# First feed-forward product of two batches as seven block products for eight, its weight blocks streamed from DRAM, with all engines in written order

## The chip, the core and the metric

The kernel runs on one core of a Trainium2 chip. A core has TensorE (PE in the profile; its weight loads are the row PEld), VectorE (DVE), ScalarE (ACT), GpSimd (POOL) and SyncE (SP), whose queue issues the transfers here. The metric is the device time of one execution in microseconds. "Granted clock" is the share of TensorE's full clock that the chip allowed in a stretch; the two levels are 1.2 and 2.4 GHz.

## The reference

Attention with normalized queries and keys, then a feed-forward layer with a squared ReLU, in fp32. The two weight matrices come as 64-bit floats (a numpy product with a 64-bit scalar made them so), so the kernel also rounds them to 32 bits.

```
# q, k, v: (8, 12, 448, 64); w_in: (768, 2048); w_out: (2048, 768)
q_n, k_n = rmsnorm(q, g_q), rmsnorm(k, g_k)       # over the last axis
scores = (1 / sqrt(64)) * q_n @ k_n^T
attn = exp(scores - max(scores)); attn /= sum(attn) + 1e-9
x = (attn @ v), laid out as (8 * 448, 12 * 64)
g = max(x @ w_in, 0) ** 2
out = g @ w_out                                   # (3584, 768)
```

## The kernel before

The work goes by batch (8) and, in a batch, by pair of heads (6). A pair's q and k come with 112 partitions; `norm` squares them and scales them by the reciprocal root of their mean (POOL, with one sum on DVE), `transposes` brings them into `qkT` with PE and DVE, `scores` makes four tiles of 112 x 2 x 448 scores with one exponential each on ACT (`pr`), `values` multiplies them with v, and POOL adds the four tiles up (`acc`), so that `finish` can get the totals with two matmuls (`tot`), take the reciprocal and write the normalized, transposed output `xT` of the batch.

`feed_forward` of a batch is a generator: 16 pieces of the first product (`ph`, six matmuls of 128x128 weights on 448 columns, then ReLU on ACT and a square in place on POOL into `gT`), then the second product (`po`, 16 matmuls of 384 columns a piece) with its rows copied out by DVE and ACT and stored. Its pieces are dealt out between the half pairs of the next batch's attention; the last batch's feed-forward runs alone. Both weights lie in SBUF as `w1` and `w2`. They are loaded as 64-bit words in 32 pieces, three at a time, and rounded in `round_weights` during the first batch's attention: exponent and fraction are put together on DVE and ACT, and multiplied on POOL.

PE runs in the written order; on the other engines and the queue a scheduler chooses the order. One row of an order listing with `MATMUL` is a matmul of the program; the trace shows two instructions for each fp32 matmul, and one for each transpose.

Of the kernel before, what the change touches and what calls it, by code (L numbers as in the profile page):

```python
# [9 lines left out]
F32 = mybir.dt.float32  # L10
# [294 lines left out]
def attention_then_ffn_bounded(  # L305
# [24 lines left out]

    nc = tc.nc
# [4 lines left out]
    P = 128  # L336
# [5 lines left out]
    REST = S % P  # L342
    FULL = S - REST
    assert 2 * D == P and S % NJ == 0 and SP <= P and B % 2 == 0
    assert DM == H * D and NT == B * S and 2 * REST == P and DFF % 512 == 0
# [3 lines left out]
    work = ctx.enter_context(tc.tile_pool(name="work", bufs=2))  # L349
    small = ctx.enter_context(tc.tile_pool(name="small", bufs=4))  # L350
    ps_s = ctx.enter_context(tc.tile_pool(name="ps_s", bufs=2, space=bass.MemoryType.PSUM))
# [10 lines left out]
    rebias = consts.tile([P, 1], F32, name="rebias")  # L362
# [6 lines left out]
    NW = 768  # L369
    NSET = 3  # L370
    spare = gT.rearrange("p f n -> p (f n)")
    assert NSET * 3 * NW <= NFC * (S + REST)
# [3 lines left out]
    CW = NPAIR // 2  # L376
    FW = NW // CW
    pieces_w = [(w1[:, c:c + CW, f:f + FW], w1r[:, c:c + CW, words_in * f:words_in * (f + FW)])
                for f in range(0, DFF, FW) for c in (0, CW)]
    pieces_w += [(w2[:, c:c + 1, :], w2r[:, c:c + 1, :]) for c in range(NFC)]  # L380

    def raw(n):
        _, a, m = pieces_w[n][0].shape
        at = n % NSET * 3 * NW
        words = spare[:, at:at + 2 * NW].bitcast(U32)
        return words.rearrange("p (a m) -> p a m", a=a), words.rearrange("p (a m two) -> p a m two", a=a, two=2)

    def load_weights(n):
        if n < len(pieces_w):
            nc.sync.dma_start(raw(n)[0] if doubles else pieces_w[n][0], pieces_w[n][1])  # L390

    def round_weights(n):
        if not doubles:
            return
        w = pieces_w[n][0]
        wu = w.bitcast(U32)
        words = raw(n)[1]
        low, high = words[:, :, :, 0], words[:, :, :, 1]
        at = n % NSET * 3 * NW + 2 * NW
        f = spare[:, at:at + NW].rearrange("p (a m) -> p a m", a=w.shape[1])  # L400
        fu = f.bitcast(U32)
        nc.vector.tensor_scalar(wu, high, 20, 0x7FF, ALU.logical_shift_right, ALU.bitwise_and)
        nc.scalar.activation(wu, wu, AF.Relu, bias=rebias)
        nc.vector.tensor_scalar(fu, high, 0xFFFFF, None, ALU.bitwise_and)
        nc.vector.scalar_tensor_tensor(f, low, 2.0 ** -32, fu, ALU.mult, ALU.add)
        nc.scalar.activation(f, f, AF.Copy, bias=1.0, scale=2.0 ** -20)
        nc.vector.tensor_scalar(wu, wu, 255.0, 2.0 ** 23, ALU.min, ALU.mult)  # L407
        nc.vector.scalar_tensor_tensor(wu, high, 0x80000000, wu, ALU.bitwise_and, ALU.bitwise_or)  # L408
        nc.gpsimd.tensor_tensor(w, f, w, ALU.mult)


    qks, vs, qkTs, probs, pavs, accs, xTs = {}, {}, {}, {}, {}, {}, {}
# [14 lines left out]
    normed = {}  # L427

    def norm(i):
        qk = qks.pop(i)  # L430
        qkn = work.tile([SP, 2, NJ, 2, D], F32, tag="qkn", name="qkn", bufs=1)
# [16 lines left out]
    def transposes(i):  # L448
        qkn = normed.pop(i)
        qkT = work.tile([P, 2, S], F32, tag="qkT", name="qkT")  # L450
# [8 lines left out]
    def scores(i, c):  # L459
# [10 lines left out]
        if c == 1:  # L470
            accs[i] = work.tile([SP, 2, S], F32, tag="acc", name="acc")
            nc.gpsimd.tensor_tensor(accs[i], probs[i, 0], pr, ALU.add)  # L472
        elif c > 1:
            nc.gpsimd.tensor_tensor(accs[i], accs[i], pr, ALU.add)  # L474
# [3 lines left out]
    def values(i, cs):  # L478
# [8 lines left out]
    def finish(i):  # L487
        b, hp = divmod(i, NPAIR)
        acc = accs.pop(i)
        tot = ps_o.tile([P, S], F32, tag="t", name="tot")  # L490
        for h in range(2):
            nc.tensor.matmul(tot[h * D:(h + 1) * D, :], ones, acc[:, h, :], start=True, stop=True)  # L492
        rec = work.tile([P, S], F32, tag="rec", name="rec", bufs=1)
        nc.vector.reciprocal(rec, tot)  # L494
        if hp == 0:
            xTs[b] = work.tile([P, NPAIR, S], F32, tag="xT", name="xT")
        nc.vector.tensor_tensor(xTs[b][:, hp, :].rearrange("d (p j) -> d j p", j=NJ),  # L497
                                pavs.pop(i).rearrange("d (j p) -> d j p", j=NJ),
                                rec.rearrange("d (j p) -> d j p", j=NJ), ALU.mult)
        del vs[i]  # L500

    def feed_forward(b):
        xT = xTs.pop(b)
        odd = b % 2
        c0 = 0 if odd else REST
        for f in range(NFC):  # L510
            ph = ps_m.tile([P, S], F32, tag="m", name="ph")
            for c in range(NPAIR):
                nc.tensor.matmul(ph, w1[:, c, f * P:(f + 1) * P], xT[:, c, :],  # L513
                                 start=(c == 0), stop=(c == NPAIR - 1))
            g = gT[:, f, c0:c0 + S]
            nc.scalar.activation(g, ph, AF.Relu)  # L516
            nc.gpsimd.tensor_tensor(g, g, g, ALU.mult)  # L517
            yield
        for t in range(0, FULL + P * odd, P):
            osb = work.tile([P, DM], F32, tag="osb", name="osb")  # L520
            for half in range(2):
                cols = slice(half * HALF, (half + 1) * HALF)
                po = ps_m.tile([P, HALF], F32, tag="m", name="po")
                for f in range(NFC):
                    nc.tensor.matmul(po, gT[:, f, c0 + t:c0 + t + P], w2[:, f, cols],  # L525
                                     start=(f == 0), stop=(f == NFC - 1))
                if half == 0:
                    nc.vector.tensor_copy(osb[:, cols], po)  # L528
                else:
                    nc.scalar.copy(osb[:, cols], po)  # L530
                if half == 1:
                    if t < FULL:
                        nc.sync.dma_start(out[b * S + t:b * S + t + P, :], osb)
                    else:
                        nc.sync.dma_start(out[b * S + FULL:(b + 1) * S, :], osb[0:REST])
                        nc.sync.dma_start(out[(b - 1) * S + FULL:b * S, :], osb[REST:P])
                yield

    def pieces(b):
        return NFC + 2 * (FULL // P + b % 2)  # L540
# [8 lines left out]
    for n in range(NSET):  # L549
        load_weights(n)  # L550
    make_identity(nc, ident)
    nc.gpsimd.memset(mhalf, -0.5)
    nc.gpsimd.memset(rebias, -896.0)
# [5 lines left out]
    NP = B * NPAIR  # L559
    for b in range(B):  # L560
        fill = feed_forward(b - 1) if b else iter(())
        n = pieces(b - 1) if b else 0
        done = 0
        blocks = 2 * NPAIR
        for u in range(blocks):
            i, second = b * NPAIR + u // 2, u % 2
            if not second:
                if i + 2 < NP:
                    load(i + 2)
                scores(i, 0)  # L570
                scores(i, 1)
                if i + 1 < NP:
                    norm(i + 1)
                if u:
                    values(i - 1, (2, 3))
                    finish(i - 1)
            else:
                if i + 1 < NP:
                    load_v(i + 1)
                    transposes(i + 1)  # L580
                scores(i, 2)
                scores(i, 3)
                values(i, (0, 1))
            if b == 0:
                m = len(pieces_w)
                for n_w in range(m * u // blocks, m * (u + 1) // blocks):
                    round_weights(n_w)
                    load_weights(n_w + NSET)
            if u == blocks - 1:
                values(i, (2, 3))  # L590
                finish(i)
            while done < n * (u + 1) // blocks:
                next(fill)
                done += 1
        for _ in fill:
            pass
    for _ in feed_forward(B - 1):
        pass
# [3 lines left out]
def kernel(  # L602
# [31 lines left out]
    with tc.If(bits <= limit) as small_scores:  # L634
        with tc.manual_schedule(engines={mybir.EngineType.PE}):
# [33 lines left out]
```

## Time and profile before

| | us |
|---|---|
| median of 3 runs (lowest to highest) | 1854.67 (1854.55 to 1856.01) |
| the profiled execution | 1852.34 |
| its span from first to last instruction | 1850.5 |
| PE busy in the span | 1624.2 (88%) |
| POOL busy | 833.4 (45%) |
| DVE busy | 496.7 (27%) |
| ACT busy | 304.4 (16%) |
| mean granted TensorE clock | 0.944 |

Busy time is a mean over stages. Which engine sets the end of a stage is read from the stretches, the chain that ended last (followed back from the last instruction to what released each step), and the idle time in front of an instruction, with the engine that ended it. Ends of matmuls are modelled, so the distance from start to start is the safer measure on PE.

### The profile page before, as it was taken

The page shows a single profiled execution, that of the slowest core. Times are in us where ns is not written, and L with a number is a line of the kernel's source. Part 1 is how long each engine was busy: PE and PEld are TensorE (multiplying, and loading weights), DVE is VectorE, ACT ScalarE, POOL GpSimd, SP SyncE. Part 2 cuts the span into 40 slices and gives each one's busy share as a digit, 9 for nine tenths or more (in the row PEclk, how much of TensorE's full clock was granted, in tenths as well). Part 3 has the DMA queues.
Part 4 walks back from the last instruction along what each step waited for, and adds up shares of the span by engine and source line. Part 5 has one row for each costly group of instructions (what it writes and reads, how often), then busy time and mean ns, then how long its engine had stood idle before and what let it go on. Part 6 is the DMA issues. An engine that isn't in the chain of part 4 may idle for free.

```text
span 1850.5 us, 13250 instructions
## 1 busy us (share of the span) xinstructions
PE 1624.2 (88%) x5440; PEld 804.5 (43%) x5440; DVE 496.7 (27%) x432; ACT 304.4 (16%) x413; POOL 833.4 (45%) x553
## 2 busy tenths in 40 slices
PE   3242479998999899998999899998999899999998
PEld 1111134454445444454445454454445454455555
DVE  6898941211211211211211212211211212210000
ACT  2333322101120011201120011201120011200100
POOL 6777676622662236622662236622663235601200
PEclk9657679998999999999999999999999999999999
DMA  5433400000100100000100100000100100000000
GB/s 157 135 119 116 148 25 25 20 33 24 30 25 24 37 24 21 25 33 24 30 26 24 37 24 17 29 32 24 30 25 24 37 24 15 10 18 9 0 10 27
DMA packets 47754, 70.16 MB, mean 38 GB/s; under 512 B 3652, under 2 KB 35908, under 8 KB 47684
## 3 DMA queue, kind: packets, MB, share of 16 engines
q1 hardware_dynamic: 47684, 69.22, 12.0%
q8 instruction: 44, 0.72, 0.2%
q14 instruction: 26, 0.21, 0.0%
HBM read 58.20 MB, written 11.01 MB: 37 GB/s over the span
## 4 chain that ended last, share of the span: by engine, by line
PE 81%; POOL 4%; DVE 2%; ACT 1%; issue 0%; POOLq 0%; ACTq 0%
PE po L525 32%; PE ph L513 32%; PE sc L465 7%; PE pav L484 6%; PE tot L492 2%; POOL acc L474 2%; PE pt L454 1%; POOL rstd L439 1%; ACT gT L516 1%; POOL qkn L441 1%; POOL qkn L434 1%; DVE rstd L437 0%; DVE w L407 0%; ACT osb L530 0%; DVE w L408 0%
## 5 line engine op out<-in xcount | busy, mean ns | idle before, releaser
L513 PE MATMUL ph<-xT,w 128*128 128x448 f32 x1536 | 595.6, 544 | 7.6 <-DVE xT L497 7.6
L525 PE MATMUL po<-w,gT 128*128 128x384 f32 x1792 | 592.3, 492 | 0.0
L525 PEld LDWEIGHTS po<-w,gT 128*128 128x128 f32 x1792 | 342.5, 192 | 256.0 <-issue 27.5
L513 PEld LDWEIGHTS ph<-xT,w 128*128 128x128 f32 x1536 | 287.5, 190 | 314.1 <-issue 305.6
L494 DVE RECIPROCAL rec<-tot 128x448 f32<-128x448 f32 x48 | 141.9, 2956 | 554.5 <-PE tot L492 554.5
L517 POOL TENSOR_TENSOR gT<-gT 128x448 f32<-128x448 f32 x128 | 118.3, 933 | 293.9 <-ACT gT L516 293.9
L465 PE MATMUL sc<-qkT 64*112 64x448 f32 x768 | 188.5, 614 | 60.1 <-DVE qkT L456 60.1
L472 POOL TENSOR_TENSOR acc<-pr 112x896 f32<-112x896 f32 x48 | 102.8, 2141 | 287.3 <-ACT pr L468 287.1
L474 POOL TENSOR_TENSOR acc<-acc,pr 112x896 f32<-112x896 f32 x96 | 201.1, 2095 | 27.5 <-ACT pr L468 27.1
L468 ACT ACTIVATE pr<-sc 112x896 f32<-112x896 f32 x192 | 166.9, 913 | 157.5 <-PE sc L465 157.5
L434 POOL TENSOR_TENSOR qkn<-qk 112x1024 f32<-112x1024 f32 x48 | 91.5, 1907 | 201.9 <-PE pt L454 191.7
L516 ACT ACTIVATE gT<-ph 128x448 f32<-128x448 f32 x128 | 69.7, 544 | 596.4 <-PE ph L513 596.4
L484 PE MATMUL pav<-pr,vt 112*64 112x448 f32 x768 | 167.4, 561 | 0.0
L456 DVE TENSOR_SCALAR qkT<-pt,gains 128x448 f32<-128x448 f32 x96 | 65.3, 682 | 340.0 <-PE pt L454 338.9
L454 PE MATMUL pt<-ident,qkn 112*128 112x112 f32 x384 | 62.1, 289 | 98.0 <-POOL qkn L441 88.5
L439 POOL TENSOR_TENSOR rstd<-rstd,mhalf 112x16 f32<-112x16 f32 x48 | 139.7, 2911 | 3.8
L465 PEld LDWEIGHTS sc<-qkT 64*112 64x112 f32 x768 | 67.1, 189 | 141.8 <-issue 133.5
L530 ACT COPY osb<-po 128x384 f32<-128x384 f32 x28 | 13.4, 479 | 682.3 <-PE po L525 682.3
L528 DVE COPY osb<-po 128x384 f32<-128x384 f32 x28 | 15.6, 558 | 349.2 <-PE po L525 349.2
L441 POOL TENSOR_TENSOR qkn<-qk,rstd 112x512 f32<-112x512 f32 x96 | 101.7, 1063 | 3.6
L454 PEld LDWEIGHTS pt<-ident,qkn 112*128 112x128 f32 x384 | 45.3, 153 | 132.2 <-POOL qkn L441 83.0
L484 PEld LDWEIGHTS pav<-pr,vt 112*64 112x64 f32 x768 | 48.3, 139 | 115.1 <-issue 90.2
(27 smaller groups left out, 497.4 us busy)
## 6 DMA issues: line engine op xcount, KB each, us to landing
gT<-in_moe_w_in_dram SPq DMA_DIRECT2D x16, 768.0 KB, 4.8
gT<-in_moe_w_out_dram SPq DMA_DIRECT2D x16, 768.0 KB, 4.3
qk<-in_q_dram SPq DMA_DIRECT2D x48, 224.0 KB, 2.9
qk<-in_k_dram SPq DMA_DIRECT2D x48, 224.0 KB, 3.2
vt<-in_v_dram SPq DMA_DIRECT2D x48, 224.0 KB, 2.7
out_dram<-osb SPq DMA_DIRECT2D x24, 384.0 KB, 2.3
out_dram<-osb SPq DMA_DIRECT2D x8, 192.0 KB, 2.7
gains<-in_g_q_dram SPq DMA_DIRECT2D x2, 0.2 KB, 2.9
```

Of the source, the lines that this page charges most:

```text
L434: nc.gpsimd.tensor_tensor(sq, flat, flat, ALU.mult)
L439: nc.gpsimd.tensor_tensor(rflat, rflat, mhalf, ALU.pow)
L441: nc.gpsimd.tensor_tensor(qkn[:, s].rearrange("p j h d -> p h j d"), qk[:, s].rearrange("p h (j d) -> p h j d", d=D), rstd[:, s].rearrange ...
L454: nc.tensor.transpose(pt[:, j * SP:(j + 1) * SP], qkn[:, s, j].rearrange("p h d -> p (h d)"), ident[:SP, :SP])
L465: nc.tensor.matmul(sc[:, h, 0:S], qkT[rows, 1, c * SP:(c + 1) * SP], qkT[rows, 0, :], start=True, stop=True)
L468: nc.scalar.activation(pr, sc[:, :, 0:S], AF.Exp)
L474: nc.gpsimd.tensor_tensor(accs[i], accs[i], pr, ALU.add)
L484: nc.tensor.matmul(pavs[i][h * D:(h + 1) * D, :], vs[i][:, h, c, :], pr[:, h, :], start=(c == 0), stop=(c == NJ - 1))
L494: nc.vector.reciprocal(rec, tot)
L513: nc.tensor.matmul(ph, w1[:, c, f * P:(f + 1) * P], xT[:, c, :], start=(c == 0), stop=(c == NPAIR - 1))
L517: nc.gpsimd.tensor_tensor(g, g, g, ALU.mult)
L525: nc.tensor.matmul(po, gT[:, f, c0 + t:c0 + t + P], w2[:, f, cols], start=(f == 0), stop=(f == NFC - 1))
```

## The change

Two batches make a span. With the weights cut in two halves each way (rows and columns of `w_in`) and the output of attention cut by features and by batch, the first product is a 2 x 2 block product; it is written with 7 block products and 15 additions (Strassen's scheme in Winograd's form). Four differences of the inputs are made on DVE in `finish` (`xC`, and a part of `xT` in place). The seven weight operands of each of 8 block rows (four of them differences, made on POOL) are written once to a DRAM tensor `w1s`, and read back one block (128 x 384) per product through six buffers `sw`. The additions of the results run on DVE, between PSUM and SBUF; three PSUM banks are accumulated into a second time.

A span's attention now runs beside the second product of the span before, cut into single matmuls, 200 of 224 over the 24 half pairs; the first product runs with nothing beside it, except the norm and transposes of one pair and, in the first span, the rounding of `w_out`. At the start, two batches' attention runs beside the rounding of `w_in`; there PE makes the totals from all four probability tiles. The square of `norm` and the copy to `qkT` go to ACT, one of three sums of probabilities to DVE. Every engine and the queue keep the written order.

```diff
-    w1 = consts.tile([P, NPAIR, DFF], F32, name="w1")
...
-    gT = consts.tile([P, NFC, S + REST], F32, name="gT")
+    gT = consts.tile([P, NFC, 2 * S], F32, name="gT")
+    xT = consts.tile([P, 2, NPAIR, S], F32, name="xT")
+    xC = consts.tile([P, 3, HC, S], F32, name="xC")
...
+    def exponents(words, w):
+        wu = w.bitcast(U32)
+        nc.vector.tensor_scalar(wu, pairs_of(words)[1], 20, 0x7FF, ALU.logical_shift_right, ALU.bitwise_and)
+        nc.scalar.activation(w, wu, AF.Relu, bias=clamp1, scale=-1.0)
+        nc.scalar.activation(wu, w, AF.Relu, bias=clamp2, scale=-(2.0 ** 23))
+    def fractions(words, w):
+        low, high = pairs_of(words)
+        wu = w.bitcast(U32)
+        f = low.bitcast(F32)
+        nc.vector.scalar_tensor_tensor(wu, high, 0x80000000, wu, ALU.bitwise_and, ALU.bitwise_or)
+        nc.vector.tensor_scalar(high, high, 0xFFFFF, None, ALU.bitwise_and)
+        nc.vector.scalar_tensor_tensor(f, low, 2.0 ** -32, high, ALU.mult, ALU.add)
+        nc.scalar.activation(f, f, AF.Copy, bias=1.0, scale=2.0 ** -20)
...
+        if step == 2 and n % 2:
+            nc.gpsimd.tensor_tensor(b[S1], b[A21], b[A22], ALU.add)
+            nc.gpsimd.tensor_tensor(b[S2], b[S1], b[A11], ALU.subtract)
+            nc.gpsimd.tensor_tensor(b[S3], b[A11], b[A21], ALU.subtract)
+            nc.gpsimd.tensor_tensor(b[S4], b[A12], b[S2], ALU.subtract)
+        if step == 3 and n % 2:
+            nc.sync.dma_start(w1s[n // 2].rearrange("k p m -> p k m"), w1_blocks(n)[:, 0:7])
...
+    def load_blocks(upto):
+        while len(stream) < min(upto, NSPAN * HF * 7):
+            n = len(stream)
+            sw = loads.tile([P, HC, P], F32, tag="sw", name="sw", bufs=6)
+            nc.sync.dma_start(sw.rearrange("p c m -> p (c m)"), w1s[n // 7 % HF, n % 7])
+            stream.append(sw)
...
-        nc.gpsimd.tensor_tensor(sq, flat, flat, ALU.mult)
+        nc.scalar.activation(sq, flat, AF.Square)
...
-            nc.vector.tensor_scalar(qkT[:, s], pt, gains[:, s:s + 1], None, ALU.mult)
+            nc.scalar.activation(qkT[:, s], pt, AF.Copy, scale=gains[:, s:s + 1])
...
+            nc.gpsimd.tensor_tensor(accs[i], probs[i, 0], pr, ALU.add)
+        else:
+            (nc.vector if c == 2 else nc.gpsimd).tensor_tensor(accs[i], accs[i], pr, ALU.add)
...
+        if t:
+            sub = nc.vector.tensor_tensor
+            if hp < HC:
+                sub(xC[:, 0, hp], xT[:, 1, hp], xT[:, 0, hp], ALU.subtract)
+            else:
+                n = hp - HC
+                sub(xC[:, 1, n], xT[:, 1, hp], xC[:, 0, n], ALU.subtract)
+                sub(xC[:, 2, n], xT[:, 0, hp], xC[:, 1, n], ALU.subtract)
+                sub(xT[:, 1, n], xT[:, 1, hp], xT[:, 1, n], ALU.subtract)
...
+        def product(ps, n, rhs, first):
+            load_blocks(n + 6)
+            for c in range(HC):
+                nc.tensor.matmul(ps, stream[n][:, c], rhs[:, c], start=first and c == 0,
+                                 stop=c == HC - 1, skip_group_check=not first)
...
+            pa = ps_o.tile([P, S], F32, tag="t", name="pa")
+            product(pa, n + A11, B11, True)
+            p1 = work.tile([P, S], F32, tag="p1", name="p1")
+            nc.scalar.copy(p1, pa)
+            yield
+            pb = ps_m.tile([P, S], F32, tag="m", name="pb")
+            product(pb, n + S2, T2, True)
+            z = work.tile([P, S], F32, tag="z", name="z")
+            add(z, p1, pb, ALU.add)
+            yield
...
+            product(pd, n + S3, T3, True)
+            add(g22, y, pd, ALU.add)
+            activate(g22, g22)
+            yield
+            product(pa, n + A12, B21, False)
+            activate(g11, pa)
+            yield
+            product(pd, n + A22, T4, False)
+            add(g21, z, pd, ALU.add)
+            activate(g21, g21)
...
+    for span in range(NSPAN):
...
+            for u, _ in enumerate(first_product(work, span)):
+                if span == 0:
+                    for n in range(4 * u // 7, 4 * (u + 1) // 7):
+                        for step in range(3):
+                            make_w2(n - step, step)
+                if more and u == 7 * (HF - 2):
+                    norm(nxt)
+                if more and u == 7 * (HF - 1):
+                    transposes(nxt)
...
+                each, done = (2 * S // P) * 2 * NFC - 24, 0
+                for u, _ in enumerate(attention(work, span + 1, False)):
+                    while done < each * (u + 1) // NB:
+                        next(rest)
+                        done += 1
...
-        with tc.manual_schedule(engines={mybir.EngineType.PE}):
+        with tc.manual_schedule():
```

In the middle of the kernel before, PE's order for one pair of heads beside the feed-forward of the batch before is this (`pt` transposes, `sc` scores, `pav` values, `tot` totals, `ph` first product):

```order
L454 MATMUL pt<-ident,qkn 128x112 x8
L465 MATMUL sc<-qkT 112x448 x4
L484 MATMUL pav<-pr,vt 64x448 x4
L513 MATMUL ph<-xT,w_100 128x448 x12
L465 MATMUL sc<-qkT 112x448 x4
L484 MATMUL pav<-pr,vt 64x448 x4
L492 MATMUL tot<-acc,ones 64x448 x2
```

After the change, PE's order for one pair of heads in the second span's attention, with the semaphores that an instruction waits for:

```order
L577 MATMUL tot<-acc,ones 64x448 [waits Pool_49]
L577 MATMUL tot<-acc,ones 64x448
L690 MATMUL po<-w_99,gT 128x384 x8
L534 MATMUL pt<-ident,qkn 128x112 [waits DVE_49,Pool_49]
L534 MATMUL pt<-ident,qkn 128x112 x3
L534 MATMUL pt<-ident,qkn 128x112 [waits Activation_49,Pool_49]
L534 MATMUL pt<-ident,qkn 128x112 x3
L545 MATMUL sc<-qkT 112x448 x4
L566 MATMUL pav<-pr,vt 64x448 [waits DMAHW5_49,DVE_49]
L566 MATMUL pav<-pr,vt 64x448 x3
L690 MATMUL po<-w_99,gT 128x384 x6
```

Between the half pairs stand some eight matmuls of the second product where there were two pieces of the feed-forward, and the second four transposes wait for ACT besides POOL.

On ACT, early in the first batch, the order before is this (L403 and L406 the two weight steps of a piece, L468 exponentials):

```order
L403 ACTIVATE w_100<-w_100,rebias 128x3x256
L406 ACTIVATE gT<-gT 128x768
L468 ACTIVATE pr<-sc 112x896 x2
L406 ACTIVATE gT<-gT 128x768
L468 ACTIVATE pr<-sc 112x896
L403 ACTIVATE w_100<-w_100,rebias 128x3x256 x2
```

On ACT, in the first span, the order after the change around one pair (L536 copies to `qkT`, L548 exponentials, L514 the square of `norm`, L391, L392 and L402 the three weight steps of one piece):

```order
L548 ACTIVATE pr<-sc 112x896 x2
L514 ACTIVATE qkn<-qk 112x1024
L391 ACTIVATE gT<-gT,clamp_103 128x768
L392 ACTIVATE gT<-gT,clamp_104 128x768
L402 ACTIVATE gT<-gT 128x768
L536 ACTIVATE qkT<-pt,gains 128x448 x2
L548 ACTIVATE pr<-sc 112x896 x2
L391 ACTIVATE gT<-gT,clamp_103 128x768
L392 ACTIVATE gT<-gT,clamp_104 128x768
L402 ACTIVATE gT<-gT 128x768
```

The copies of a pair now stand behind the weight steps of the half pair before it; before, a scheduler put single weight steps between the exponentials, and ACT had neither the copies nor the squares of the attention.

On SP, around the end of the first span's attention after the change (`w1s` the store of weight blocks, `gT<-in_moe_w_out` a piece of the second weights, `sw` a block):

```order
L506 DMA vt<-in_v_dram 112x2x256
L460 DMA w1s<-gT 128x7x384
L468 DMA gT<-in_moe_w_out_dram 128x1536 x3
L490 DMA sw<-w1s 128x384 x11
L468 DMA gT<-in_moe_w_out_dram 128x1536
L490 DMA sw<-w1s 128x384
L468 DMA gT<-in_moe_w_out_dram 128x1536
```

The first blocks stand behind the last store and three pieces of the second weights; all of these are new at this place.

## Rows read from the trace of the kernel before

**Rows 1.** Busy time by stretch: start to end, engines, then clock, DMA share, GB/s.
```profile
0.00:245.00 245.00, 89.88 (x292) 34.72 (x292) 211.19 (x198) 77.96 (x91) 173.46 (x96) 0.70 0.41 127
245.00:1689.00 1444.00, 1379.12 (x4700) 684.65 (x4700) 283.30 (x231) 215.29 (x301) 645.01 (x442) 0.98 0.08 26
```

**Rows 2.** Chain that ended last: start, length, instructions (us).
```profile
448.16 9.23 PE ph L513 x24
...
865.45 9.23 PE ph L513 x24
...
1689.53 72.16 PE ph L513 x192
1761.69 82.57 PE po L525 x256
```

**Rows 3.** Timeline of PE, 525 to 540 us: start, length, instructions, idle before.
```profile
525.33 1.76 PE L465 MATMUL sc<-qkT 64*112 64x448 f32 x8
527.02 1.72 PE L484 MATMUL pav<-pr,vt 112*64 112x448 f32 x8
528.58 0.92 PE L492 MATMUL tot<-acc,ones 112*64 112x448 f32 x4
529.43 9.29 PE L513 MATMUL ph<-xT,w 128*128 128x448 f32 x24
...
539.35 0.60 PE L454 MATMUL pt<-ident,qkn 112*128 112x112 f32 x4 [0.25 <-ACT gT L516]
```

**Rows 4.** Timeline of PE at the end of a batch's attention.
```profile
840.20 1.76 PE L492 MATMUL tot<-acc,ones 112*64 112x448 f32 x4 [7.95 <-POOL acc L474]
```

**Rows 5.** Groups of attention's instructions by line: busy us, mean ns of one.
```profile
L468 ACT ACTIVATE pr<-sc 112x896 f32<-112x896 f32 x192 | 166.9, 913 | 157.5 <-PE sc L465 157.5
L494 DVE RECIPROCAL rec<-tot 128x448 f32<-128x448 f32 x48 | 141.9, 2956 | 554.5 <-PE tot L492 554.5
L439 POOL TENSOR_TENSOR rstd<-rstd,mhalf 112x16 f32<-112x16 f32 x48 | 139.7, 2911 | 3.8
...
L441 POOL TENSOR_TENSOR qkn<-qk,rstd 112x512 f32<-112x512 f32 x96 | 101.7, 1063 | 3.6
...
L516 ACT ACTIVATE gT<-ph 128x448 f32<-128x448 f32 x128 | 69.7, 544 | 596.4 <-PE ph L513 596.4
...
L456 DVE TENSOR_SCALAR qkT<-pt,gains 128x448 f32<-128x448 f32 x96 | 65.3, 682 | 340.0 <-PE pt L454 338.9
...
L437 DVE TENSOR_REDUCE rstd<-qkn 112x16 f32<-112x1024 f32 x48 | 58.5, 1218 | 60.6 <-POOL qkn L434 60.6
...
L497 DVE TENSOR_TENSOR xT<-pav,rec 128x448 f32<-128x448 f32 x48 | 46.1, 961 | 1.5
...
L438 POOL TENSOR_SCALAR rstd<-rstd 112x16 f32<-112x16 f32 x48 | 11.6, 242 | 56.9 <-DVE rstd L437 56.4
```

**Rows 6.** DMA issues: tensors, count, size of one, median us to landing.
```profile
gT<-in_moe_w_in_dram SPq DMA_DIRECT2D x16, 768.0 KB, 4.8
...
qk<-in_q_dram SPq DMA_DIRECT2D x48, 224.0 KB, 2.9
```

**Rows 7.** Timeline of the start: first exponential; eight score instructions near 211 us.
```profile
20.92 0.92 ACT L468 ACTIVATE pr<-sc 112x896 f32<-112x896 f32 x1 [1.52 <-PE sc L465]
...
211.54 3.33 PE L465 MATMUL sc<-qkT 64*112 64x448 f32 x8
```

**Rows 8.** Groups of the weights' instructions by line: busy us, mean ns of one.
```profile
L405 DVE SCALAR_TENSOR_TENSOR gT<-gT 128x768 f32<-128x768 uint32 x32 | 41.9, 1308 | 0.0
L408 DVE SCALAR_TENSOR_TENSOR w<-gT,w 128x768 uint32<-128x768 uint32 x32 | 39.3, 1228 | 0.0
L404 DVE TENSOR_SCALAR gT<-gT 128x768 uint32<-128x768 uint32 x32 | 30.0, 937 | 0.0
L403 ACT ACTIVATE w<-w,rebias 128x768 uint32<-128x768 uint32 x32 | 29.4, 932 | 34.0 <-DVE w L402 34.0
...
L406 ACT ACTIVATE gT<-gT 128x768 f32<-128x768 f32 x32 | 26.9, 841 | 53.8 <-DVE gT L405 53.8
```

More of the change, by code (lines that the diff above doesn't have):

```diff
@@ L414, in load @@
+    stream = []
+    def load_blocks(upto):
[4 more added lines that the diff above has]
+            stream.append(sw)
+    qks, vs, qkTs, probs, pavs, tots, accs, normed = {}, {}, {}, {}, {}, {}, {}, {}
     def load(i):
@@ L449, in transposes @@
         qkn = normed.pop(i)
-        qkT = work.tile([P, 2, S], F32, tag="qkT", name="qkT")
+        qkT = loads.tile([P, 2, S], F32, tag="qkT", name="qkT")
         for s in range(2):
@@ L485, in values, with sums, finish @@
                                  start=(c == 0), stop=(c == NJ - 1))
-    def finish(i):
+            if pe_sums:
+                sums(i, pr, c == 0, c == NJ - 1)
+        if not pe_sums and NJ - 1 in cs:
+            sums(i, accs.pop(i), True, True)
+    def sums(i, pr, first, last):
+        if first:
+            tots[i] = ps_o.tile([P, S], F32, tag="t", name="tot")
+        for h in range(2):
+            nc.tensor.matmul(tots[i][h * D:(h + 1) * D, :], ones, pr[:, h, :], start=first, stop=last)
+    def finish(work, i):
         b, hp = divmod(i, NPAIR)
[L489 to L492, printed above, removed]
+        t = b % 2
         rec = work.tile([P, S], F32, tag="rec", name="rec", bufs=1)
[L494 to L497, printed above, removed]
+        nc.vector.reciprocal(rec, tots.pop(i))
+        nc.vector.tensor_tensor(xT[:, t, hp, :].rearrange("d (p j) -> d j p", j=NJ),
                                 pavs.pop(i).rearrange("d (j p) -> d j p", j=NJ),
@@ new lines, in attention @@
+    def attention(work, span, pe_sums):
+        first, end = 2 * span * NPAIR, 2 * (span + 1) * NPAIR
+        for i in range(first, end):
+            if i + 2 < B * NPAIR:
+                load(i + 2)
+            scores(work, i, 0, pe_sums)
+            scores(work, i, 1, pe_sums)
+            if i + 1 < end:
+                norm(i + 1)
+            if i > first:
+                values(i - 1, (2, 3), pe_sums)
+                finish(work, i - 1)
+            yield
+            if i + 1 < B * NPAIR:
+                load_v(i + 1)
+            if i + 1 < end:
+                transposes(i + 1)
+            scores(work, i, 2, pe_sums)
+            scores(work, i, 3, pe_sums)
+            values(i, (0, 1), pe_sums)
+            if i == end - 1:
+                values(i, (2, 3), pe_sums)
+                finish(work, i)
+            yield
@@ L520, in feed_forward, with second_product @@
+    chunks = [f for f in range(NFC) if f % HF < HF - 1] + [HF - 1, NFC - 1]
+    def second_product(work, span):
+        for t in range(0, 2 * S, P):
             osb = work.tile([P, DM], F32, tag="osb", name="osb")
@@ L523, in feed_forward @@
                 po = ps_m.tile([P, HALF], F32, tag="m", name="po")
[L524 to L540, printed above, removed]
+                for f in chunks:
+                    nc.tensor.matmul(po, gT[:, f, t:t + P], w2[:, f, cols],
+                                     start=(f == chunks[0]), stop=(f == chunks[-1]))
+                    if f == chunks[-1]:
+                        if half == 0:
+                            nc.vector.tensor_copy(osb[:, cols], po)
+                        else:
+                            nc.scalar.copy(osb[:, cols], po)
+                            nc.sync.dma_start(out[2 * span * S + t:2 * span * S + t + P, :], osb)
+                    yield
     load(0)
@@ L557, in attention_then_ffn_bounded @@
     transposes(0)
[L559 to L596, printed above, removed]
```

182 lines of the change are left out of this document (117 added, 65 removed).

## Prediction

> **What bounds the kernel now.** I read the busy time by stretch first. In the first 245 us [rows 1] TensorE (PE) works 90 us at a mean granted clock of 0.70, while VectorE (DVE) is busy 211 us and GpSimd (POOL) 173 us: that stretch rounds all 32 weight pieces and runs one batch's attention, and PE waits. From 245 to 1689 us PE is busy 1379 of 1444 us at 0.98: PE sets the end, and a microsecond comes off only where PE gets less work or loses a wait. Second the chain that ended last [rows 2]: one feed-forward without attention takes 72.16 us for 192 instructions of the first product (0.376 us each; a matmul of the program is two instructions) and 82.57 us for 256 of the second (0.3225 us each). From the same point of one batch pair to the next (448.16 to 865.45) are 417.3 us. Third the timeline: in attention eight score instructions take 1.69 us from start to start, eight value instructions 1.56, four sums 0.85, four transposes 0.60 [rows 3], so a pair of heads costs PE 2 x 1.69 + 2 x 1.56 + 0.85 + 2 x 0.60 = 8.55 us; I use 8.6. Last, each batch's end has a hole: PE waits 7.95 us for POOL's sum of the probabilities [rows 4], after the filling pieces have run out.
>
> **The first product.** 8 blocks of 2 x 3 matmuls become 7 for each pair of row blocks: 4 x 8 x 7 x 3 x 2 = 1344 instructions for 1536. The form (128x128 weights, 448 columns) is unchanged, so 192 x 0.376 = 72.2 us of PE work go away; per span of two batches 336 x 0.376 = 126.3 us stay. What comes beside it: five DVE adds per seven products. The trace has no such add; a 128x448 DVE instruction with a PSUM operand takes 0.68 us (L456), a two-operand one 0.96 (L497) [rows 5]. I take 0.8: 4.0 us in 7 x 2.256 = 15.8, hidden. Each sum has a whole product (2.26 us) before its bank is written again, also at 0.96. ScalarE (ACT) gets one copy more (0.54, L516). If that cover went, each product would end with about 0.9 us of waiting.
>
> **The stream.** A block is 192 KB, asked for five products (11.3 us) before its use. q and k transfers of 224 KB land in 2.9 us, weight pieces of 768 KB in 4.8 [rows 6]; 192 KB per 2.256 us is 87 GB/s, where the first stretch moved 127 [rows 1]. I take nothing for it. The Trainium skill (DMA: Bandwidth & Descriptors, "Anatomy of one DMA") speaks against it: on the path it describes a DMA costs about 2.0 us plus its bytes at 436 GB/s. That is an estimated 2.45 us for a block, and blocks served one after another would then pace the product, 224 x 0.19 = 43 us more. The trace has no stream like this one and shows only that transfers land in a time above that.
>
> **Attention beside the second product.** Only the second product fills now: 200 of 224 matmuls over 24 half pairs, 8.33 of them (16.7 x 0.3225 = 5.4 us) each; before, a filling piece was 12 or 32 instructions and two went into most half pairs. So the norm of the next pair has less time. From the first score of a pair: score 0.85, two exponentials of 0.91, a square on ACT of about 1.04 (0.913 x 1024/896), the sum on DVE 1.22, on POOL 0.24 + 2.91, then two scalings of 1.06 [rows 5]; with 0.1 us per hand-over the first scaled half is there at about 9.7 us, the second at 10.7. PE gets there after 1.69 + 1.56 + 0.85 + 5.4 = 9.5 us. The second transpose moreover waits for ACT's copy of the first (its wait names ACT): only one bank is free while a second product stands open. 9.8 + 0.55 + 0.2 + 0.55 + 0.1 = 11.2 us in place of 10.1. I take 1.0 us of waiting in 11 pairs, and 4 in the first pair of a span, where no values precede: 15 us a span. Bounds: nothing (norm 1.2 us faster), and 3 us a pair (the square at 1.2, DVE or POOL late by another 1). A span's stage is 12 x 8.6 + 144.5 + 15 - 1.2 (one pair's transposes lie in the first product) = 261.5 us. The hole of rows 4 goes: the last 24 matmuls (15.5 us) cover the last reciprocal (2.96), product and differences.
>
> **The start.** It now holds two batches' attention, 16 weight pieces for 32, and every engine in written order. First exponential at 21 us as before [rows 7]. The loop of a pair, from its first exponential: exponentials and square to 2.9 on ACT; sum, power and scalings to 9.4; on DVE the reciprocal starts when the sums are there (6.5), with the product ends at 10.5, and only then come the weight steps: exponents 0.94 (as L404, of the same form), then 1.23 + 0.94 + 1.31 [rows 8], to 14.9. ACT stands in that order too: two clamps (0.93 each) from 11.4, the copy (0.84) from 14.9 to 15.8, and only then the next pair's two qkT copies (1.1), two exponentials (1.8) and the second half's three weight steps (2.7): 21.5. PE at the low clock (16 score instructions 2 x 3.33 us [rows 7]) needs some 20 itself. I take 22.5 for the six pairs with weight steps in both halves, 19 for the four with one, 30 for first and last: 135 + 76 + 30 = 241. With 21 in front, 7 for the differences on DVE (12 x 0.6 in the second batch, a form like L456's) and 5 until the first block lands behind three 768 KB loads: 274 us, where before 245 us held one batch. Bounds: 16 us a pair, the norm chain and PE alone, 218; 26 in the heavy pairs and a late block, 310. POOL's products and differences of weights (384 elements; L441 takes 1.06 us for 512) lie behind its scalings, in time that it has.
>
> **The second half of the weights** runs beside the first span's product: four pieces per seven products cost DVE 4 x (0.94 + 1.23 + 0.94 + 1.31) + 4.0 = 21.7 us against PE's 15.8, for four groups: 4 x 5.9 = 24 us. The means of rows 8 come from a stretch with POOL busy 7 of 10; I take 15, with 0 and 25 as bounds. Behind a waiting DVE add stands the next bank, and so PE.
>
> **Sum.** Start 274; first span's product 126.3 + 1.2 + 15 = 142.5; three stages of 261.5 = 784.5; two products of 127.5 and the last of 126.3 = 381.3; the last second product 448 x 0.3225 = 144.5; from the last matmul to the end 6.2 (1761.69 + 82.57 = 1844.3 [rows 2], to 1850.5). Together 1733 us of span, against 1850.5. Around the span lie 1.8 us, and the median shown is 2.3 over the profiled execution: **1737 us**.
>
> **Rivals.**
> Both waits hidden: the start at 235 and no waiting at the transposes (1733 - 39 - 33): some 1665. For it: PE never waited at its transposes in the middle of a batch in rows 3 beyond 0.25 us. Against: half the filling work.
> Attention waits 3 us a pair, not 1: 33 x 2 = 66 more, about 1803. For it: four engines in written order in one chain; against: the whole chain to the second scaling is 10.7 us of a pair of 8.6 + 10.8.
> The sums pace the first product, so that seven products take as long as eight did (18 us a span): 1809. It would need 2.58 us per product from a DVE that works 4 us in 15.8.
> The other side, slower: blocks land one after another. At the 2.9 us of rows 6 for each of 224 blocks it is 224 x 0.64 = 144 us more, 1881; it decides from 2.77 us per block. For it: one queue, and stores, weights and blocks on it. Against: six buffers, and the 127 GB/s of the first stretch. The skill's price for a block, above, would end at about 1780, inside the forecast's range.
>
> **How the numbers follow.** The forecast, 1700 to 1790 with its own bounds, 0.62; both hidden (1640 to 1700) 0.16; long waits 0.13; sums as pace 0.04; stream one by one 0.05 (0.01 of it within 0.2% of before). Leaving about a tenth on each side gives 1680 to 1815. This kernel can tell 0.2% (3.7 us) from no change. Faster 0.95, same 0.01, slower 0.04.
>
> **What would show it.** 1344 first-product instructions at 0.376 us, a span's product in 126 to 128 us from the second on; PE waiting about 1 us at the second transpose for ACT, no 8 us hole; first-product matmuls starting between 230 and 310 us; DVE over nine tenths busy in the first span's product; blocks landing well before use. Wrong it goes if ACT or DVE queues wait for each other longer than worked out, above all at the start, which is the least certain term, or if PE waits for blocks.

## Result, and the profile after

The changed kernel takes 1774.53 us (median of 4, 1773.27 to 1775.95) against 1855.28 beside it: 0.9565 of the time, 95% interval 0.9548 to 0.9582. The span of the profiled execution falls from 1850.5 to 1774.0 us, the granted clock rises from 0.944 to 0.957. The forecast was 1737, the range 1680 to 1815.

Busy time by stretch of the changed kernel, cut at the start, the first span's product, the attention beside its second product, and the second span's first product (columns as in [rows 1]):

```profile
0.00:277.80 277.80, 166.43 (x673) 64.56 (x673) 150.11 (x113) 109.97 (x133) 146.76 (x122) 0.80 0.41 132
277.80:450.90 173.10, 139.84 (x346) 67.67 (x346) 95.68 (x108) 66.18 (x90) 69.61 (x51) 0.90 0.38 123
450.90:715.10 264.20, 252.11 (x970) 122.95 (x970) 86.62 (x67) 69.21 (x88) 109.31 (x70) 0.99 0.14 41
715.10:842.90 127.80, 127.36 (x345) 64.38 (x343) 25.35 (x40) 24.37 (x43) 33.95 (x35) 1.00 0.31 89
```

The last stretch is what Strassen was to give: its 336 product instructions take 127.8 us, PE busy all of it, the stream moving 89 GB/s. The last second product is alone on PE as in [rows 2] (chain: start, length, instructions), and the blocks land sooner than the transfers of [rows 6]:

```profile
1623.91 144.50 PE po L690 x448
```
```profile
sw<-w1s SPq DMA_DIRECT2D x224, 192.0 KB, 2.4
```

The wait of [rows 4] for POOL's sum is down to 0.6 us. Over the run, PE's waits for that sum (us in total, times, longest) before, and after with the wait at the second transposes:

```profile
PE tot L492 <- POOL acc L474: 54.4, 9, 7.9
```
```profile
PE pt L534 <- ACT qkT L536: 22.0, 27, 0.8
...
PE tot L577 <- POOL acc L556: 1.8, 3, 0.6
```

But the second stretch is the first span's product, of the same instructions, and takes 45 us more; DVE, the busiest engine after PE, works 96 of its 173 us. Who waits there (us in total, times, longest), engines first, then SP's queue:

```profile
PE pd L636 <- DVE z L656: 23.3, 4, 6.9
...
DVE w L389 <- DMA gT<-in_moe_w_out_dram: 18.2, 9, 5.5
```
```profile
SPq L468 <- POOL w L480: 54.9, 13, 6.1
```

PE waits for DVE's add, DVE for a load of `w_out`, and SP's queue for POOL, which must have read the word buffer before it is loaded again. The chain that ended last shows one turn of this loop (start, length, what):

```profile
297.29 2.54 POOL w L480
299.85 4.24 DMA gT<-in_moe_w_out_dram
304.09 0.02 issue
304.11 0.56 DVE w L389
304.67 0.88 DVE w L399
305.55 0.02 issue
305.57 0.57 DVE gT L400
306.14 0.02 issue
306.17 0.97 DVE gT L401
307.13 0.02 issue
307.16 0.91 ACT gT L402
308.07 0.07 issue
308.14 1.85 POOL w L480
310.00 4.56 DMA gT<-in_moe_w_out_dram
```

And the timelines of DVE, ACT and PE with it:

```profile
304.11 0.56 DVE L389 TENSOR_SCALAR w<-gT 128x768 uint32<-128x768 uint32 x1 [5.48 <-DMA gT<-in_moe_w_out_dram]
...
308.50 0.62 DVE L656 TENSOR_TENSOR z<-p,pb 128x448 f32<-128x448 f32 x1 [1.38 <-ACT p L651]
```
```profile
307.96 0.51 ACT L651 COPY p<-pa 128x448 f32<-128x448 f32 x1
```
```profile
309.18 4.27 PE L636 MATMUL pd<-xT,sw 128*128 128x448 f32 x6 [6.87 <-DVE z L656]
313.28 2.42 PE L636 MATMUL pa<-xT,sw 128*128 128x448 f32 x6
```

`z` (L656) stands behind the steps of two pieces in DVE's written order, these behind a load, and `pd` needs the bank that `z` reads. What ends the wait of `z` here is ACT: its copy `p` (L651), which `z` reads, stands behind L402 of the same piece in ACT's written order. After the wait the six instructions take 4.27 us, the next six 2.42; the granted clock of the stretch is 0.90.

The stages of all kernels that were run, each from the first matmul of the stage to that of the next (us; attention is the mean of its three stretches, later product that of the second and third span):

| kernel | median | until first product | first span's product | attention + second product | later product |
|---|---|---|---|---|---|
| forecast | 1737 | 274 | 142.5 | 261.5 | 127.5 |
| changed | 1774.53 | 277.8 | 173.0 | 263.6 | 127.9 |
| e1 four word buffers | 1763.15 | 274.9 | 162.1 | 263.6 | 127.9 |
| e2 words spread | 1737.22 | 275.9 | 135.2 | 264.5 | 127.9 |
| e3 eight products | 1805.17 | 254.1 | 168.9 | 262.5 | 147.2 |
| e4 only PE in written order | 1699.30 | 262.9 | 129.6 | 258.0 | 127.9 |
| e5 all but SP | 1772.39 | 273.9 | 172.5 | 263.6 | 127.9 |
| e6 PE and SP | 1673.53 | 214.1 | 149.6 | 258.0 | 127.9 |
| e7 filling between | 1741.31 | 274.4 | 173.4 | 252.7 | 127.9 |
| e8 = e4 + e7 | 1704.96 | 263.4 | 129.7 | 259.5 | 127.9 |
| e9 norm early | 1775.56 | 274.4 | 174.7 | 264.5 | 127.9 |
| e10 = e2 + e7 + e9 | 1703.87 | 274.8 | 135.3 | 253.3 | 127.9 |
| e11 two block buffers | 1862.86 | 275.0 | 214.6 | 264.0 | 142.8 |
| e12 = e10 + third block set | 1690.81 | 260.8 | 135.4 | 253.4 | 127.9 |

### The profile page after: what moved, and what is told of

Same layout as the page of the kernel before. It is cut to its first block, busy times and chain, and to the rows that moved or that the text cites. A ratio compares the mean times of both kernels' runs of the same rounds, so it can differ in the third digit from the quotient of the medians.

```text
span 1774.0 us, 14261 instructions
## 1 busy us (share of the span) xinstructions
PE 1586.6 (89%) x5392; PEld 778.4 (44%) x5392; DVE 585.1 (33%) x548; ACT 458.7 (26%) x621; POOL 642.2 (36%) x482
## 4 chain that ended last, share of the span: by engine, by line
PE 73%; POOL 8%; DVE 6%; ACT 5%; issue 4%; DMA 3%; SPq 0%; POOLq 0%; ACTq 0%; DVEq 0%
PE po L690 31%; PE sc L545 8%; PE pd L636 7%; PE pc L636 7%; PE pa L636 7%; PE pav L566 6%; PE pb L636 3%; POOL rstd L519 2%; PE pt L534 2%; POOL qkn L521 2%; ACT pr L548 2%; PE tot L577 2%; DMA gT<-in_moe_w_out_dram 1%; DVE rstd L517 1%; ACT qkT L536 1%
## 5 line engine op out<-in xcount | busy, mean ns | idle before, releaser
L690 PEld LDWEIGHTS po<-w,gT 128*128 128x128 f32 x1792 | 334.5, 190 | 269.1 <-issue 51.0
L548 ACT ACTIVATE pr<-sc 112x896 f32<-112x896 f32 x192 | 166.1, 914 | 226.6 <-PE sc L545 226.6
L517 DVE TENSOR_REDUCE rstd<-qkn 112x16 f32<-112x1024 f32 x48 | 58.5, 1220 | 315.9 <-ACT qkn L514 315.9
L636 PE MATMUL pa<-xT,sw 128*128 128x448 f32 x384 | 156.8, 545 | 5.5 <-DVE rec L585 3.1
L554 POOL TENSOR_TENSOR acc<-pr 112x896 f32<-112x896 f32 x36 | 75.4, 2094 | 214.0 <-ACT pr L548 214.0
L556 POOL TENSOR_TENSOR acc<-acc,pr 112x896 f32<-112x896 f32 x36 | 74.8, 2079 | 168.7 <-DVE acc L556 158.4
L640 ACT ACTIVATE gT<-gT 128x448 f32<-128x448 f32 x96 | 55.2, 575 | 300.0 <-DVE gT L665 186.8
L536 ACT ACTIVATE qkT<-pt,gains 128x448 f32<-128x448 f32 x96 | 59.6, 632 | 270.0 <-PE pt L534 270.0
L636 PEld LDWEIGHTS pa<-xT,sw 128*128 128x128 f32 x384 | 73.1, 191 | 78.8 <-issue 69.4
L636 PE MATMUL pd<-xT,sw 128*128 128x448 f32 x192 | 84.8, 581 | 23.3 <-DVE z L656 23.3
L556 DVE TENSOR_TENSOR acc<-acc,pr 112x896 f32<-112x896 f32 x36 | 39.3, 1092 | 157.5 <-ACT pr L548 157.5
```

What stands on the lines that cost most here:

```text
L536: nc.scalar.activation(qkT[:, s], pt, AF.Copy, scale=gains[:, s:s + 1])
L548: nc.scalar.activation(pr, sc[:, :, 0:S], AF.Exp)
L556: (nc.vector if c == 2 else nc.gpsimd).tensor_tensor(accs[i], accs[i], pr, ALU.add)
L636: nc.tensor.matmul(ps, stream[n][:, c], rhs[:, c], start=first and c == 0, stop=c == HC - 1, skip_group_check=not first)
L690: nc.tensor.matmul(po, gT[:, f, t:t + P], w2[:, f, cols], start=(f == chunks[0]), stop=(f == chunks[-1]))
```

## Experiments

Each was timed beside the kernel before (medians 1853.5 to 1854.3).

**e1, a fourth buffer for the words of `w_out`.** The last piece's words are overwritten by a sum before they are used, so the last 128 rows of `w_out` are not the reference's; the work is the same.

```diff
-        f = (HF - 2, NFC - 2, HF - 4)[n % SETS]
+        f = (HF - 2, NFC - 2, HF - 4, NFC - 4)[n % 4]
...
-            load_w2(n + SETS)
+            load_w2(n + 4)
```

> The loads of w_out get a fourth buffer (rows 12 and 13 of gT), so that a piece is asked for two steps ahead and not one; DVE, ACT and POOL do the same work in the same order. Theory A (a load of 4.2 us is asked for only one step before it is needed, and the adds of the block products stand behind it on DVE): the weights beside the first span's product take about 85 to 90 us and not 102, the product 156 to 162 and not 173, the kernel 1757 to 1764. Rival B (DVE's work, slowed by POOL, is itself the bound): no change, 1771 to 1777, and DVE's waits for the loads turn into nothing that PE gains. Rival C (PE is slow there because its clock is low and the blocks share the DMA with the weights): no change either, with PE's waits for DVE gone but its matmuls as slow.

The product takes 162.1 us, as theory A gave it. DVE's 18.2 us of waiting for loads are gone, but PE still waits for `z`:

```profile
PE pd L636 <- DVE z L656: 20.3, 4, 5.2
```

So the late load is 11 us of the 45, not all.

**e2, the pieces over 51 products, DVE's steps one at a time.** `fractions` is cut in two, and three of five word buffers lie in the pool of the product.

```diff
-                    for n in range(4 * u // 7, 4 * (u + 1) // 7):
-                        for step in range(3):
-                            make_w2(n - step, step)
+                    if u % 3 == 0:
+                        make_w2(u // 3, 0)
+                        make_w2(u // 3 - 2, 3)
+                    else:
+                        make_w2(u // 3 - 1, u % 3)
```

> The 16 pieces of w_out run over 51 of the 56 products (one per three products and not four per seven), with five word buffers, and DVE's steps of a piece are dealt to three products one by one, so that no burst is longer than 2.1 us. All the work stays. Theory A and rival B both say that PE's waits for z go: the first span's product 128 to 131 us, the kernel 1729 to 1735. Rival C: the product stays above 140 us, the kernel above 1741, with the low clock or waits for blocks in it.

135.2 us with the same work: 27 more are gone, and the kernel is 37 us faster than the changed one (the product 4 us and the kernel 2 us above what was expected). The longest wait of PE that is left in that stretch, and the stretch:

```profile
PE pd L646 <- DVE z L666: 2.6, 1, 2.6
```
```profile
276.00:411.00 135.00, 132.02 (x344) 66.20 (x344) 84.24 (x108) 65.18 (x90) 72.10 (x51) 0.97 0.50 168
```

The clock there rises to 0.97 as the waits go, so rival C took, in the main, an effect for the cause. Between A and B the loss divides: 11 us for loads asked for too late (e1), 27 for too much DVE work in too few products, in bursts ahead of `z` (e2), some 7 left. e2 changes the spacing of the pieces, the length of the bursts and the number of buffers at once, so its 27 us are not divided among these. Of the 7 left, 3 are waits; the rest is PE at a lower clock, 0.80 in the first 14 us, behind a wait of 3.8 us for the first block, and again after the wait for `z`.

**e3, Strassen taken out.** Four streamed blocks, each used twice; no sums, no differences, and four blocks stored for seven.

```diff
             product(pa, n + A11, B11, True)
...
+            product(pb, n + A11, B12, True)
...
             product(pa, n + A12, B21, False)
             activate(g11, pa)
...
+            product(pb, n + A12, B22, False)
+            activate(g12, pb)
```

> Strassen alone is taken out: eight block products from the four blocks of the weights, no sums and differences, all else (two batches to a span, streamed blocks, weights in two halves, written order) as changed. If the seven products for eight are the gain: the later first products 145 us for 128 (18 each), the start 5 to 15 us shorter (no sums on POOL, no differences on DVE), the first span's product 150 to 165, the kernel 1785 to 1825. Rival (the gain came from the rest, the order and the filling): 1770 to 1780.

1805.17: seven products for eight are worth 30.6 us in this arrangement, not 72. The later products pay what was worked out and a little more (147.2 for 127.9, three times: 57 us with the last), but the start gives 24 back without POOL's sums, DVE's differences and three sevenths of each store, more than I had allowed:

```profile
0.00:254.10 254.10, 164.42 (x672) 64.00 (x672) 132.27 (x102) 110.09 (x133) 108.99 (x90) 0.81 0.40 125
```

POOL is busy 109 us there, for 147 with the sums. The profiled execution took 1801.22 us, so the stages add up to 25 us and not to the 30.6 of the medians.

**e4, only PE in written order, as before the change.**

```diff
-        with tc.manual_schedule():
+        with tc.manual_schedule(engines={mybir.EngineType.PE}):
```

> Only PE is kept in written order, as before the change; the other engines' order is a scheduler's, which puts nearly all steps of w_out ahead of the first block product, among the attention of the start. So the first span's product is 126 to 129 us, and the start holds 16 pieces of 4.4 us of DVE work more: if DVE sets the start, it grows by 45 to 70 us, and the kernel takes 1775 to 1800. Rival (the start waits for something else than DVE's work, so that the pieces go into its gaps): start plus 10 to 30, the kernel 1740 to 1760.

Both missed: 1699.30. Of the 16 pieces of `w_out` 15 now lie in the start (the last ends 7 us into the product), and it is still 15 us shorter than without them; DVE's work went into its gaps. The first span's product, with almost nothing beside it, is 129.6, and each attention stretch is 5.7 us shorter.

```profile
0.00:262.90 262.90, 158.10 (x673) 60.40 (x673) 187.80 (x174) 149.34 (x179) 184.76 (x141) 0.84 0.56 181
```

The written order of the other engines and of the queue, a part of the change, costs 75 us.

**e5 and e6, which queue's order.** e5 names PE, ACT, DVE and POOL in the same line, e6 PE and SP.

> PE, ACT, DVE and POOL in written order as changed, the order of SP's loads and stores a scheduler's (q, k and v of the next pairs ahead of the loads and stores of weights that wait for POOL). Theory S (the start is long because q, k and v stand in SP's queue behind weight transfers): the start until the first block product falls from 275-278 to 250-262 us, the kernel 1750 to 1765; the first span's product stays at 165 to 173, since a word buffer is still free only after POOL's product. Theory E (it is the written order of the computing engines, each waiting in turn for the next): start and kernel as changed, 1765 to 1780.

> PE and SP in written order, ACT, DVE and POOL in a scheduler's. Theory S: the start stays at 268 to 280; theory E: it falls to 250-262. In both the adds of the first span's product are no longer behind weight steps whose load has not landed, so that the product takes 128 to 150 us and the kernel 1725 to 1755 by S, 1705 to 1735 by E.

SP's order alone is worth nothing (1772.39), so theory S falls. The computing engines' order is worth 101 us (1673.53, the fastest kernel here, 0.9034 of before, 0.9019 to 0.9050), far more than theory E's own span: by the table 64 in the start, 23 in the first span's product and 17 in the three attention stretches. With those engines scheduled, SP's written order is the better one by 26 us (e4 to e6). What PE waits for most in the start, in the changed kernel (until 277.8 us) and then in e6 (until 214):

```profile
PE pt L534 <- POOL qkn L521: 101.9, 22, 15.8
```
```profile
PE pav L566 <- issue: 38.3, 11, 5.1
PE pt L534 <- POOL qkn L521: 21.5, 4, 15.3
```

**e7, filling between the two groups of transposes.**

```diff
             nc.scalar.activation(qkT[:, s], pt, AF.Copy, scale=gains[:, s:s + 1])
+            if between and s == 0:
+                between()
...
+                def between():
+                    nonlocal done
+                    for _ in range(3):
+                        next(rest)
+                        done += 1
```

> In the attention beside the second product three filling matmuls (0.97 us) are put between a pair's two groups of transposes; the filling per half pair is otherwise the same. Theory (the second group waits for ACT's copy of the first, since only one PSUM bank is free): the 27 waits of 0.8 us for ACT's copy go, 264 us a stage become 256 to 258, the kernel 1751 to 1757. Rival (the norm of the next pair is late, and the wait only shows at the second group): the wait turns into one for POOL's scaled q and k, the kernel 1768 to 1776.

Measured 1741.31, more than the theory's own price. In the changed kernel PE's timeline shows the wait, 0.25 us in [rows 3], in nearly each pair:

```profile
564.30 0.60 PE L534 MATMUL pt<-ident,qkn 112*128 112x112 f32 x4
565.72 0.57 PE L534 MATMUL pt<-ident,qkn 112*128 112x112 f32 x4 [0.82 <-ACT qkT L536]
```

It is gone in e7, and a stretch takes 252.2 for 264.2 us. Of these 12, 8.9 are waits that the two traces list (12.0 and 3.1); PE's busy time is 3.1 less for the same instructions. About half of that goes with the clock: 0.99 in this stretch, 1.00 in e7, and the changed kernel's middle stretch, at 1.00, takes 262.5. The rest is open.

**e8, the same on e4.**

> The same filling between the transposes, with only PE in written order as in e4. By the theory 11 waits of 0.74 us go in each of three stages: e4's 1699 less 20 to 24 us, 1675 to 1680. By the rival 1695 to 1702.

It gains nothing (1704.96 for 1699.30), against both: the wait has moved. PE in the first attention stretch, POOL in one pair of it, and POOL in a pair of e7:

```profile
PE tot L579 <- POOL acc L558: 9.9, 12, 1.0
```
```profile
550.10 2.91 POOL L519 TENSOR_TENSOR rstd<-rstd,mhalf 112x16 f32<-112x16 f32 x1
553.09 2.04 POOL L521 TENSOR_TENSOR qkn<-qk,rstd 112x512 f32<-112x512 f32 x2
555.09 2.08 POOL L558 TENSOR_TENSOR acc<-acc,pr 112x896 f32<-112x896 f32 x1
```
```profile
541.72 2.07 POOL L558 TENSOR_TENSOR acc<-acc,pr 112x896 f32<-112x896 f32 x1 [5.69 <-DVE acc L558]
...
550.61 2.91 POOL L519 TENSOR_TENSOR rstd<-rstd,mhalf 112x16 f32<-112x16 f32 x1
```

The scheduler puts the next pair's norm ahead of the last sum, for which the totals wait; in e7's written order the sum ends before the norm begins. So with this filling written order is the better one here (252.7 us a stretch for 259.5), without it the worse one (263.6 for 258.0), and in the start it is the worse one.

**e9, the norm half a pair earlier in the start.**

```diff
-            if i + 1 < end:
+            if i + 1 < end and not (pe_sums and i > first):
                 norm(i + 1)
...
+            if pe_sums and i + 2 < end:
+                norm(i + 2)
```

> All engines in written order as changed; in the start alone the norm of the next pair is written half a pair earlier, ahead of a half's weight steps, and so goes through ACT, DVE and POOL before them. Theory E (in the start each engine stands in written order, and the norm's chain over ACT, DVE and POOL comes too late for the transposes, so that PE waits 102 us for POOL's scaled q and k): most of the 86 us of these waits beyond the first goes, the start falls from 275-278 to 215-240 us, the kernel 1712 to 1740. Rival (the weights' own round of load, DVE, ACT, POOL sets the start whatever the norm does): 1765 to 1778.

Theory E's first form falls: 1775.56. The waits for POOL do shrink from 101.9 to 25 us, and PE waits for ACT in their place:

```profile
PE sc L545 <- ACT pr L548: 74.4, 10, 12.3
PE pt L534 <- POOL qkn L521: 25.0, 5, 15.6
```

ACT in turn waits for the weights' steps. In the changed kernel's timeline:

```profile
136.24 0.38 SPq L460 DMA_DIRECT2D w1s<-gT  x1
...
142.97 0.56 DVE L389 TENSOR_SCALAR gT<-gT 128x768 uint32<-128x768 uint32 x1 [10.63 <-DMA w1s<-gT]
...
143.57 0.94 ACT L391 ACTIVATE gT<-gT,clamp 128x768 f32<-128x768 uint32 x1 [7.61 <-DVE gT L389]
...
146.02 0.90 ACT L402 ACTIVATE gT<-gT 128x768 f32<-128x768 f32 x1 [0.55 <-DMA qk<-in_q_dram]
146.81 1.72 ACT L548 ACTIVATE pr<-sc 112x896 f32<-112x896 f32 x2
```

DVE waits for the store of finished blocks, since the next exponents go into the same buffer; the exponentials stand behind on ACT.

**e10 and e11, the three edits together, and two buffers for the stream.**

```diff
-            sw = loads.tile([P, HC, P], F32, tag="sw", name="sw", bufs=6)
+            sw = loads.tile([P, HC, P], F32, tag="sw", name="sw", bufs=2)
...
-            load_blocks(n + 6)
+            load_blocks(n + 2)
```

> The three edits of e2, e7 and e9 together, all engines in written order. If each acts in its own stage, their gains add up: start as in e9 (215 to 240), first span's product 130 to 136, attention stages 252, later products as before: 1640 to 1668. Rival: what one stage gives another takes back (the weights of the start late for the blocks, or the words of w_out late): 1685 or more.

1703.87: e2 and e7 add up exactly (37.3 + 33.2 off 1774.5 is 1704.0), e9 adds nothing. The time lies in the rival's span, but not by its mechanism: no stage takes back what another gave; the start was not shortened at all.

> The streamed blocks get two buffers for six, and are asked for two products ahead: a block's transfer can start only when the product before it has ended, and has one product (2.256 us) to land. If a transfer alone takes the 2.4 us that the changed kernel's profile shows, each product waits 0.2 to 0.6 us: the later first products 138 to 162 us for 128, the kernel 1805 to 1880. The Trainium skill (DMA: Bandwidth & Descriptors, Anatomy of one DMA) would give an estimated 2.45 us, the same. Rival (a transfer alone lands faster than 2.2 us, and the 2.4 us hold a wait in the queue behind other blocks): 128 us stay, the kernel 1770 to 1780.

1862.86, 0.5% behind the kernel before. A later product takes 142.5 us in the second span, 2.54 for each block: that is the round of one block when no transfer overlaps another (2.3 us from issue to landing, and the hand-over). The Trainium skill (DMA: Bandwidth & Descriptors, "Anatomy of one DMA") gives an estimated 2.45 us on the path that it describes, DMAs issued by GpSimd and not by SP as here; the trace's 2.3 and 2.54 lie on either side of it. With six buffers the same blocks land in 2.4 us and cost nothing, since they overlap. The later products make 47 us of the loss. Another 42 fall in the first span's product (214.6 us), where loads of `w_out`, which wait for POOL, stand in the same queue and PE waits 60 us for blocks.

**e12, a third buffer for finished blocks.**

```diff
-        at = OUTS + n // 2 % 2 * n8
+        at = OUTS + n // 2 % 3 * n8
```

> e10 with a third buffer for the finished weight blocks in the start, and nothing else. In the changed kernel the exponents of a piece are written into the block buffer whose store to DRAM is issued just before in the same step, so that DVE waits for that store, ACT for DVE, the next exponentials for ACT (in e9 DVE waits 31.8 us for it in 4 waits, and ACT 91 us for DVE). Theory W (this wait for the store sets the heavy pairs of the start, 27 us each for 18 to 19 of the light ones): four to six pairs lose 6 to 8 us, the start 274.8 becomes 220 to 245, the kernel 1650 to 1675 for e10's 1704. Rival (POOL's products and sums, which the store waits for anyway, set the pairs): start 265 to 275, the kernel 1694 to 1706.

Between the two: 13 us off e10. DVE's wait for the store, here in e10, is gone, and another, for the loads of `w_in`, is longer in its place (2.8 us of it in e10):

```profile
DVE gT L389 <- DMA w1s<-gT: 31.7, 5, 9.4
```
```profile
DVE gT L389 <- DMA gT<-in_moe_w_in_dram: 19.0, 5, 5.3
```

## Why the prediction was right, and where it was off

- **First product.** 72.2 us of PE work go, the adds and the stream are hidden: right. Later products take 127.9, 127.9 and 126.3 us for 127.5, 127.5 and 126.3; DVE's add takes 0.62 us, not 0.8.
- **Stream.** "I take nothing for it": right with six buffers; e11 shows the price without them, and the slower rival's mechanism with it.
- **Attention.** 264.2, 262.5 and 264.2 us for 261.5. The wait at the second transposes came, a little smaller than worked out: 0.8 us in 9 pairs a span (22.0 us in 27 waits over the run) for 1.0 in 11. That it goes with the bank follows from the kernel's text and fits e7, where other matmuls fill it; no run gave a second bank. With waits of 12.0 us in the first stretch for the 15 worked out, the stretch is longer by PE's own work, 252.1 us for 246.5. The rival of 3 us a pair did not come.
- **Second half of the weights.** This term is mis-sized: "I take 15, with 0 and 25 as bounds", and it was 45, beyond its bound by 20. I counted DVE's work and took what exceeds PE's time. What the runs put in its place is the order: a load asked for one step before its use (e1: 11 us) and add steps, and the ACT copy that they read, queued behind bursts of weight steps (e1 to e2: 27). The bound failed since it held only work, no waiting. DVE over nine tenths busy, as I had expected to see, was wrong for the same reason (96 of 173 us). This makes 30 of the 41 us by which the forecast span, 1733, was low; the rest is 6 in attention and 4 in the start. That the time still lies in the range is luck as far as this term goes: most of the room above 1737 was meant for the start and for long waits at the transposes.
- **The start.** 277.8 for 274: right in size, not in cause. Between pairs' first exponentials lie 18 to 28 us, but the long ones come not only from DVE's steps and ACT's order, as I worked out, but also from the store of the blocks (e12: 14 us of the start). Of the 64 us between the changed start and e6's, e12 finds 14; e9 rules out the norm's place alone. The loads of `w_in`, one step ahead like those of `w_out`, are a candidate by e12's trace (19.0 us of DVE's waiting); that was not tried, nor which of ACT's, DVE's and POOL's order matters most.
- **What the change gained.** Measured each by itself: Strassen 31 us; written order of ACT, DVE and POOL minus 101 (e6), of these and SP minus 75 (e4). By subtraction from the 81 us gained, some 125 are left for the rest: the spans of two batches, the filling by single matmuls, the steps moved between engines. No run took these alone, and the parts need not add up. One piece can be read in the traces: PE's waits for POOL's sums fall from 54.4 to 1.8 us.

## What to carry to other kernels

Where every engine keeps the written order, a step that waits for a load holds all that stands behind it: ask for the load two steps ahead, and deal the steps out so that no short add that PE needs stands behind a long burst. Bound a cost beside other work by its waits too, not only by busy time. Written order and a scheduler's order are worth trying per engine: here a scheduler's was better by 60 us in the start, and beside the second product it depended on the filling, by 6 to 7 us a stretch either way.

## What the runs showed of the hardware

DVE's one-operand step L400 takes 0.56 us alone and 2.09 beside POOL's product, here in the changed kernel:

```profile
305.57 0.56 DVE L400 TENSOR_SCALAR gT<-gT 128x768 uint32<-128x768 uint32 x1
...
316.79 2.09 DVE L400 TENSOR_SCALAR gT<-gT 128x768 uint32<-128x768 uint32 x1
```
```profile
315.90 2.56 POOL L480 TENSOR_TENSOR w<-gT,w 128x768 f32<-128x768 f32 x1
```

POOL ends at 318.46, and 0.42 us later DVE does, so DVE seems to have stood still until then. The Trainium skill (SBUF — State Buffer, "SBUF: two separate sides") says that GpSimd and some DVE operations (in a two-port mode, or with two inputs in SBUF) share a pair of ports as an exclusive lock, and that the one that comes second blocks for the whole instruction of the other; the trace agrees, but no run here shows in which mode L400 works.
